# A GELU block with its backward pass: the first block of x loaded plainly and turned by TensorE, u kept out of q's tile, new orders

## The chip, the cores and the metric

The kernel runs on 1 core of one Trainium2 chip. The metric is the device time of one execution in microseconds (us); less is better. The profile is of one further execution on the same chip.

## What is computed

With x and grad_out of 2048 x 448, w1 of 448 x 1792 and w2 of 1792 x 448, all bf16, the reference computes

```python
def _fwd_reference(x, w1, b1, w2, b2):
    h = jnp.einsum("bsd,df->bsf", x, w1) + b1
    h = _gelu(h)
    return jnp.einsum("bsf,fd->bsd", h, w2) + b2
...
    _out, _vjp = jax.vjp(_f, x, w1, b1, w2, b2)
    _grads = _vjp(grad_out)
```

where `_gelu` is the tanh approximation. There are six outputs: out, and the gradients of x, w1, b1, w2 and b2.

## The kernel before

The 2048 rows of x are cut into 4 blocks of 512 and the 1792 hidden columns into 7 pairs of 128-column tiles, so there are 28 pairs p, block by block: pair p belongs to block p // 7. For each pair the kernel does these steps, by the letters of its order lists:

- `u` (TensorE, L315): (x w1) turned, hidden columns on the partitions, 512 rows of x along the free axis, into two PSUM banks. Since 448 = 3.5 x 128, a pair runs as half-array products: `u`p.1 is 6 matmuls of 64 rows, `u`p.2 is 8, and two of them run side by side (L248). For pair 0 the block is halved instead, into `h0.0` and `h1.0`, 8 matmuls of 256 columns each (L278).
- `c` (L399): the two banks plus b1 go to SBUF, tile A on ACT and B on DVE.
- `g`, `s`, `t` on ACT (the GELU, a square, a tanh: L420, L425, L450) and `e r y z m n` on DVE (L430 to L460) make the GELU and its derivative; each works on 1024 elements per partition.
- `q` (L332): (grad_out w2^T) turned, like `u`, from gT and w2T, always into banks 6 and 7, which are one tile, `qb`.
- `G` (L465, DVE): the derivative times q, which frees `qb` for the next pair.
- `o` and `x` (L338): out and the gradient of x, one block at a time, 2 halves x 14 hidden tiles, in banks 0 to 3; `p` is such a unit of 4 matmuls for block 0's out. `vo` and `vx` (L479) evict them into three stages, `S` (L495) stores them.

The hidden activations go to DRAM (`H`, L570), the gradients of the pre-activation are turned on chip by DMA (`T`, L574). After the 28 pairs TensorE runs two long products of 14 x 16 matmuls each, for the gradients of w1 (L704) and w2 (L758).

The order is written out by hand for every engine: PE_ORDER (L91), ACT_ORDER (L112), DVE_ORDER (L119), SP_ORDER (L130), POOL_ORDER (L138). A planner (L18) only adds the waits; nothing is reordered. U_BANK (L137) gives the banks of `u`: pair 1 banks 0 and 1, pair 3 banks 6 and 7 (in `qb`), all others 4 and 5. `h1.0` also lies in 6 and 7 (L321).

The head runs so. SP issues X0.0 and X0.1, two DMA loads that turn x's first block on the way (L510, L537), and then the plain loads of w1 (`L`, and `R` for its last 64 rows: L545, L550) and w2 (`K`, L558), and further turned loads: `Y` of grad_out, `J` of w2, `X` of x, `I` of w1. Eight DMA semaphores go round, so a load waits for the landing of the one eight places before it. ACT issues L0, R0, b1 and b2 and loads its table. TensorE runs 9 idle matmuls (`W9`, L365), spreads b2 over the partitions (`B`, L589), runs one more idle matmul, then h0.0. DVE turns b1 (L606), copies b2 (L634) and one edge column (`Dx0`, L530).

Of the kernel before, what the change touches and what calls it, by code (L numbers as in the profile page):

```python
# [88 lines left out]


PE_ORDER = """  # L91
W9 B W1 h0.0 h1.0 u1.1 u2.1 u1.2 u2.2 u3.1 p0.0 p0.1 u3.2 u4.1 p0.2 p0.3 u4.2 p1.0 p1.1 p1.2 p1.3 p2.0 u5.1 p2.1 p2.2
u5.2 p2.3 p3.0 p3.1 p3.2 u6.1 p3.3 u6.2 q0.1 p4.0 p4.1 q0.2 p4.2 u7.1 p4.3 p5.0 u7.2 p5.1 p5.2 p5.3 u8.1 p6.0 p6.1
u8.2 q1.1 p6.2 p6.3 q1.2 u9.1 o1.1.0.4.1 u9.2 o1.0.0.4.1 q2.1 u10.1 q2.2 u10.2 o1.0.0.4.2 q3.1 u11.1 q3.2 u11.2
o1.1.0.4.2 o1.0.4.8.1 o1.1.4.8.1 u12.1 o1.0.4.8.2 u12.2 q4.1 o1.1.4.8.2 q4.2 u13.1 o1.0.8.11.1 u13.2 q5.1 o1.1.8.11.1
q5.2 o1.0.8.11.2 o1.1.8.11.2 o1.0.11.14.1 o1.1.11.14.1 q6.1 o1.0.11.14.2 q6.2 o1.1.11.14.2 x0.0.0.4.1 u14.1 x0.0.0.4.2
u14.2 x0.1.0.4.1 q7.1 u15.1 q7.2 u15.2 x0.1.0.4.2 x0.0.4.8.1 q8.1 u16.1 q8.2 u16.2 x0.1.4.8.1 x0.0.4.8.2 q9.1 u17.1
q9.2 u17.2 x0.1.4.8.2 x0.0.8.11.1 x0.1.8.11.1 x0.0.8.11.2 u18.1 x0.1.8.11.2 u18.2 q10.1 x0.0.11.14.1 q10.2 u19.1
x0.1.11.14.1 u19.2 q11.1 x0.0.11.14.2 q11.2 u20.1 x0.1.11.14.2 u20.2 q12.1 o2.0.0.4.1 q12.2 o2.1.0.4.1 o2.0.0.4.2
o2.1.0.4.2 o2.0.4.8.1 q13.1 o2.1.4.8.1 q13.2 o2.0.4.8.2 o2.1.4.8.2 o2.0.8.11.1 o2.1.8.11.1 q14.1 o2.0.8.11.2 q14.2  # L100
u21.1 o2.1.8.11.2 u21.2 q15.1 o2.0.11.14.1 q15.2 u22.1 o2.1.11.14.1 u22.2 q16.1 o2.0.11.14.2 u23.1 q16.2 u23.2
o2.1.11.14.2 x1.0.0.4.1 u24.1 x1.0.0.4.2 u24.2 x1.1.0.4.1 q17.1 x1.1.0.4.2 q17.2 x1.0.4.8.1 x1.1.4.8.1 x1.0.4.8.2
q18.1 x1.1.4.8.2 q18.2 x1.0.8.11.1 x1.1.8.11.1 x1.0.8.11.2 q19.1 x1.1.8.11.2 q19.2 x1.0.11.14.1 x1.1.11.14.1
x1.0.11.14.2 u25.1 x1.1.11.14.2 u25.2 q20.1 o3.0.0.4.1 q20.2 o3.1.0.4.1 u26.1 o3.0.0.4.2 u26.2 q21.1 o3.1.0.4.2 q21.2
o3.0.4.8.1 u27.1 o3.1.4.8.1 u27.2 q22.1 o3.0.4.8.2 q22.2 o3.1.4.8.2 o3.0.8.11.1 o3.1.8.11.1 q23.1 o3.0.8.11.2 q23.2
o3.1.8.11.2 o3.0.11.14.1 o3.1.11.14.1 o3.0.11.14.2 q24.1 o3.1.11.14.2 q24.2 x2.0.0.4.1 x2.1.0.4.1 x2.0.0.4.2 q25.1
x2.1.0.4.2 q25.2 x2.0.4.8.1 x2.1.4.8.1 x2.0.4.8.2 x2.1.4.8.2 x2.0.8.11.1 x2.1.8.11.1 x2.0.8.11.2 q26.1 x2.1.8.11.2
q26.2 x2.0.11.14.1 x2.1.11.14.1 x2.0.11.14.2 q27.1 x2.1.11.14.2 q27.2 x3.0.0.4.1 x3.1.0.4.1 x3.0.0.4.2 x3.1.0.4.2
x3.0.4.8.1 x3.1.4.8.1 x3.0.4.8.2 x3.1.4.8.2 x3.0.8.11.1 x3.1.8.11.1 x3.0.8.11.2 x3.1.8.11.2 x3.0.11.14.1 x3.1.11.14.1
x3.0.11.14.2 x3.1.11.14.2  # L110
"""
ACT_ORDER = """  # L112
L0 R0 b1 b2 table c0A0 c0A1 s0 g0 c1A t0 s1 g1 s2 c3A g2 c4A t1 g3 s3 c5A t2 g4 s4 s5 c6A g5 g6 c7A t3 g7 s6 c8A g8
c9A g9 t4 c10A g10 s7 t5 c11A g11 s8 c12A t6 g12 s9 c13A g13 t7 t8 c14A g14 s10 t9 c15A g15 s11 t10 c16A g16 s12 t11
c17A g17 s13 s14 c18A t12 g18 c19A g19 t13 vx0.0 vx0.1 vx0.2 c20A vx0.3 g20 s15 t14 s16 t15 s17 s18 t16 c21A g21 t17
c22A g22 s19 t18 c23A g23 s20 t19 s21 t20 s22 c24A t21 g24 vx1.0 vx1.1 vx1.2 vx1.3 s23 c25A t22 g25 s24 c26A t23 g26
s25 s26 c27A t24 g27 s27 t25 t26 t27 vx2.0 vx2.1 vx2.2 vx2.3 vx3.0 vx3.1 vx3.2 vx3.3
"""
DVE_ORDER = """  # L119
b1T b2c Dx0 c0B0 c0B1 e0 r0 y0 c1B c2A c2B z0 e1 c3B m0 r1 y1 c4B z1 e2 n0 m1 r2 y2 z2 c5B n1 m2 Dg0 n2 c6B G0 e3 r3  # L120
y3 c7B z3 m3 n3 c8B vo0.2 vo0.3 vo0.0 vo0.1 G1 e4 c9B r4 y4 z4 G2 c10B m4 e5 n4 r5 y5 z5 c11B m5 G3 n5 e6 r6 y6 c12B
z6 m6 G4 n6 e7 c13B r7 y7 z7 G5 e8 m7 r8 y8 vo1.0 vo1.1 z8 vo1.2 m8 vo1.3 G6 c14B e9 n7 r9 y9 z9 G7 c15B m9 e10 n8 r10
y10 z10 G8 c16B m10 e11 n9 r11 y11 z11 c17B m11 G9 n10 e12 n11 r12 c18B y12 z12 G10 m12 e13 c19B r13 y13 z13 G11 m13
c20B e14 n12 r14 y14 z14 G12 m14 e15 n13 r15 y15 z15 n14 G13 m15 e16 n15 r16 y16 z16 G14 m16 e17 c21B r17 y17 z17 G15
m17 c22B e18 n16 r18 y18 vo2.0 vo2.1 c23B vo2.2 vo2.3 z18 G16 m18 e19 n17 r19 y19 z19 G17 m19 e20 n18 r20 y20 z20 G18
m20 e21 n19 r21 y21 z21 c24B G19 m21 e22 n20 r22 y22 z22 c25B G20 m22 e23 n21 r23 y23 z23 c26B n22 m23 G21 n23 e24 r24
y24 z24 c27B G22 m24 e25 n24 r25 y25 z25 G23 m25 vo3.0 vo3.1 vo3.2 vo3.3 G24 e26 e27 r26 r27 y26 y27 z26 z27 m26 m27
n25 n26 G25 n27 G26 G27
"""
# [33 lines left out]
def make_plan(tc, ctx, x, w1, b1, w2, b2, grad_out, out_0, out_1, out_2, out_3, out_4, out_5):  # L163
# [420 lines left out]
    for t in PE_ORDER.split():  # L584
        k, a = t[0], t[1:]
        if k == "W":
            wake(int(a))
        elif k == "B":
            pe("b2u", lambda: nc.tensor.matmul(bk_(3)[:, 0:D], lhsT=one[0:1, 0:P], rhs=stage[NST - 1][0:1, 0, :], start=True, stop=True,  # L589
                                               skip_group_check=True), ["b2r"], [bank(("b2u",), 3)], ("s448", 1), (None, 0))  # L590
# [11 lines left out]
    pl.op("POOL", "b1z", lambda: nc.gpsimd.memset(b1n[:], 0.0), [], ["b1z"], ("tiny", 1))
# [199 lines left out]
```

## Time and profile before

| what | value |
|---|---|
| median of 3 runs | 271.16 us (270.48 to 271.91) |
| the profiled execution | 271.01 us |
| its span, from the first to the last instruction | 269.2 us |
| TensorE (PE) busy | 262.0 us, 97% of the span |
| VectorE (DVE) busy | 202.6 us, 75% |
| ScalarE (ACT) busy | 121.3 us, 45% |
| GpSimd (POOL) busy | 15.2 us, 6% |
| moved by DMA | 46.09 MB, mean 171 GB/s |

A line such as L241 is a line of the kernel. PEld is the weight load that runs beside the matmuls. In the lines of groups stand the busy time, the mean of one instruction in ns, then the idle time of the engine just before them and what ended it. The chain of waits is followed back from the last instruction, so it shows at each moment what the end was waiting for.

### The profile page before, as it was taken

What the parts mean: (1) busy time and instruction counts of PE and PEld (TensorE: products, weight loads), DVE (VectorE), ACT (ScalarE), POOL (GpSimd) and SP (SyncE); (2) the same over time, 40 slices, a digit from 0 to 9 for tenths busy, and PEclk for the clock granted to TensorE, in tenths of its full rate; (3) what the DMA queues carried; (4) which work ended last, traced back from release to release, by engine and by line L of the source; (5) the groups of instructions that cost most, each with busy time, mean ns of one, the idle gap of its engine ahead of it and who ended that gap; (6) DMA issues with size and microseconds to landing.
All of it is one profiled execution on the core that took longest, in us unless ns stands there. A gap on an engine that the chain in (4) does not pass through costs nothing.

```text
span 269.2 us, 5316 instructions
## 1 busy us (share of the span) xinstructions
PE 262.0 (97%) x2157; PEld 161.5 (60%) x2157; DVE 202.6 (75%) x286; ACT 121.3 (45%) x153; POOL 15.2 (6%) x9
## 2 busy tenths in 40 slices
...
GB/s 149 281 264 198 192 153 139 230 276 240 233 205 207 171 204 46 121 156 154 56 209 61 255 260 41 215 206 104 162 150 230 186 178 196 190 173 181 68 71 34
DMA packets 121403, 46.09 MB, mean 171 GB/s; under 512 B 98879, under 2 KB 121249, under 8 KB 121378
## 3 DMA queue, kind: packets, MB, share of 16 engines
...
q10 hardware_dynamic: 510, 0.33, 0.4%
...
## 4 chain that ended last, share of the span: by engine, by line
PE 91%; DVE 3%; ACT 2%; DMA 1%; ACTq 1%; issue 0%
PE bank L241 42%; PE qb L241 16%; PE bank L758 12%; PE bank L704 11%; PE qb L704 4%; PE qb L758 4%; DMA st<-in_b_dram 1%; ACT TR L427 1%; DVE gh_nat L411 1%; PE bank L285 1%; DVE TR L442 1%; ACTq L505 1%; PE qb L285 1%; DVE TR L457 0%; DVE TR L447 0%; DVE TR L437 0%
## 5 line engine op out<-in xcount | busy, mean ns | idle before, releaser
L241 PEld LDWEIGHTS <-HG 64*128 64x128 bf16 x896 | 62.1, 94 | 26.9 <-POOLq L236 0.8
L241 PE MATMUL qb<-gT,w2Tf 64*128 64x512 bf16 x392 | 53.7, 376 | 0.0
L241 PE MATMUL bank<-w_sb,HG 64*128 64x448 bf16 x448 | 51.6, 349 | 0.1
L241 PE MATMUL bank<-xT,w1f 64*128 64x512 bf16 x364 | 49.1, 376 | 1.6 <-DVE gh_nat L411 1.6
L241 PE MATMUL bank<-w1T_sb,HG 64*128 64x448 bf16 x448 | 48.2, 349 | 0.0
L467 DVE SCALAR_TENSOR_TENSOR HG<-TR,qb 128x1024 bf16<-128x1024 bf16 x28 | 34.1, 1218 | 7.0 <-PE qb L241 6.8
L241 PEld LDWEIGHTS <-w2Tf 64*128 64x128 bf16 x392 | 27.0, 94 | 13.4
L758 PEld LDWEIGHTS <-HG 128*128 128x128 bf16 x240 | 23.4, 98 | 19.2
L241 PEld LDWEIGHTS <-w1f 64*128 64x128 bf16 x378 | 24.2, 94 | 16.9 <-issue 2.5
L704 PEld LDWEIGHTS <-gh_nat 128*128 128x128 bf16 x224 | 21.8, 98 | 20.6 <-issue 0.4
L452 ACT ACTIVATE TR<-TR 128x1024 bf16<-128x1024 bf16 x28 | 29.3, 1048 | 10.0 <-DVE TR L442 10.0
L758 PE MATMUL bank<-w2Tf,HG 128*128 128x448 bf16 (+1 forms) x176 | 32.3, 344 | 0.0
L704 PE MATMUL bank<-w1f,gh_nat 128*128 128x448 bf16 x160 | 30.8, 353 | 0.0
L727 DVE TENSOR_TENSOR w1T_sb<-w1T_sb,gh_nat 128x1792 f32<-128x1792 f32 x14 | 28.4, 2026 | 0.5
L733 POOL PARTITION_ALL_REDUCE w1T_sb<-w1T_sb x1 | 10.6, 10649 | 206.2 <-DVE w1T_sb L731 206.2
L764 DVE CAST w_sb<-bank 128x448 bf16<-128x448 f32 x5 | 3.1, 625 | 24.8 <-PE bank L758 24.8
L427 ACT ACTIVATE TR<-gh_nat 128x1024 bf16<-128x1024 bf16 x15 | 15.8, 1055 | 10.8 <-DVE TR L462 10.6
L457 DVE TENSOR_SCALAR TR<-TR 128x2048 bf16<-128x2048 bf16 x28 | 19.2, 688 | 0.5 <-ACT TR L452 0.5
L462 DVE TENSOR_TENSOR TR<-TR 128x1024 bf16<-128x1024 bf16 x28 | 19.2, 687 | 0.1
L447 DVE TENSOR_TENSOR TR<-TR,HG 128x1024 bf16<-128x1024 bf16 x28 | 19.1, 685 | 0.0
L427 ACT ACTIVATE TR<-ub 128x1024 bf16<-128x1024 bf16 x13 | 13.7, 1055 | 10.5 <-DVE TR L462 9.9
L742 DVE TENSOR_TENSOR ub<-ub,w2Tf 128x448 f32<-128x448 f32 x14 | 16.4, 1172 | 0.5
...
## 6 DMA issues: line engine op xcount, KB each, us to landing
...
```

Source lines behind the costliest of these rows:

```text
L241: m = nc.tensor.matmul(bk_(b)[:, 0:n], lhsT=l, rhs=r, start=st, stop=sp, skip_group_check=True)
L427: pl.op("ACT", f"s{p}", lambda: nc.scalar.activation(out=TR[p % NTR][:, 1], in_=ubuf(p), func=ACT.Square, scale=sc), [("ub", p)], [v], ("a ...
L447: pl.op("DVE", f"R{p}", lambda: nc.vector.tensor_tensor(out=t[:, 1], in0=t[:, 1], in1=hblk(p), op=ALU.mult), [("r", p), ("h", p)], [val((" ...
L452: pl.op("ACT", f"t{p}", lambda: nc.scalar.activation(out=t[:, 0], in_=t[:, 0], func=ACT.Tanh), [("y", p)], [val(("t", p), ("TR0", p % NTR) ...
L457: pl.op("DVE", f"m{p}", lambda: nc.vector.tensor_scalar(out=t[:], in0=t[:], scalar1=1.0, scalar2=None, op0=ALU.subtract), [("t", p), ("r2" ...
L462: pl.op("DVE", f"n{p}", lambda: nc.vector.tensor_tensor(out=t[:, 0], in0=t[:, 0], in1=t[:, 1], op=ALU.mult), [("m0", p), ("m1", p)], [val( ...
L467: pl.op("DVE", f"G{p}", lambda: nc.vector.scalar_tensor_tensor(out=ghblk(p), in0=t[:, 0], scalar=2.0, in1=qb[:, :, :], op0=ALU.subtract, o ...
L704: nc.tensor.matmul(bk_(bk)[:, 0:D], lhsT=gh_nat[:, st // 4, ft, st % 4, :], rhs=x_nat[:, st, :], start=(st == 0), stop=(st == NS - 1))
L727: nc.vector.tensor_tensor(out=hs3, in0=a, in1=gh_nat[:, st // 4, :, st % 4, :], op=ALU.add)
L733: pl.op("POOL", "gb1", lambda: nc.gpsimd.partition_all_reduce(gb1_w, hsum, channels=P, reduce_op=bass_isa.ReduceOp.add), ["hsc"], ["gb1"], ...
L742: nc.vector.tensor_tensor(out=gsum, in0=gsum, in1=g_nat[:, st, :], op=ALU.add)
L758: nc.tensor.matmul(bk_(bk)[:, 0:d1 - d0], lhsT=h_nat[ft][:, st, :], rhs=g_nat[:, st, d0:d1], start=(st == 0), stop=(st == NS - 1))
```

## The change

x's first block is no longer loaded by turned loads. SP issues three plain loads of its rows (one tile of 128 rows, one, and two) into the third TR buffer, which is free so early; POOL writes column minus row as int32 into a stage, DVE makes an identity of it; TensorE turns each 128 x 128 piece by a product with the identity, 16 matmuls, into banks 0 to 3; DVE copies the first and the third bank into xT, ACT the second and the fourth. R0 moves from ACT to SP. The idle matmuls become 6, ahead of the turns; `B` moves behind h1.0, to bank 6.

No `u` lies in `qb` any more: h1.0 goes to banks 2 and 3, pair 2 to banks 2 and 3, pair 3 to 4 and 5.

All orders are new. From pair 4 on both evictions `c` are ACT's (24 move from DVE). The gradient of x of block 0 runs before the out of block 1, and so on in turn; q0 comes behind u5 instead of u6; the units of `o` and `x` take 5, 5 and 4 hidden tiles instead of 4, 4, 3 and 3. In SP's order `K3` moves behind `Y0` and `J0`, and `I0` and `I1` come before `Y1`.

```diff
 PE_ORDER = """
-W9 B W1 h0.0 h1.0 u1.1 u2.1 u1.2 u2.2 u3.1 p0.0 p0.1 u3.2 u4.1 p0.2 p0.3 u4.2 p1.0 p1.1 p1.2 p1.3 p2.0 u5.1 p2.1 p2.2
-u5.2 p2.3 p3.0 p3.1 p3.2 u6.1 p3.3 u6.2 q0.1 p4.0 p4.1 q0.2 p4.2 u7.1 p4.3 p5.0 u7.2 p5.1 p5.2 p5.3 u8.1 p6.0 p6.1
...
+W6 X0 X1 X2 X3 h0.0 h1.0 B u1.1 u2.1 u1.2 u3.1 u2.2 u3.2 p0.0 p0.1 u4.1 p0.2 p0.3 u4.2 p1.0 p1.1 p1.2 p1.3 u5.1 p2.0
+p2.1 u5.2 q0.1 p2.2 p2.3 q0.2 u6.1 p3.0 p3.1 u6.2 q1.1 p3.2 p3.3 q1.2 p4.0 p4.1 p4.2 p4.3 u7.1 p5.0 p5.1 u7.2 p5.2
+q2.1 p5.3 p6.0 q2.2 u8.1 p6.1 p6.2 u8.2 q3.1 p6.3 x0.1.0.5.1 u9.1 q3.2 u9.2 x0.0.0.5.1 x0.1.0.5.2 q4.1 u10.1 q4.2
+u10.2 x0.0.0.5.2 q5.1 x0.0.5.10.1 u11.1 q5.2 u11.2 x0.1.5.10.1 q6.1 u12.1 q6.2 u12.2 x0.0.5.10.2 x0.1.5.10.2 u13.1
+q7.1 u13.2 q7.2 x0.0.10.14.1 x0.1.10.14.1 x0.0.10.14.2 u14.1 q8.1 u14.2 q8.2 x0.1.10.14.2 o1.0.0.5.1 u15.1 q9.1 u15.2
+q9.2 o1.1.0.5.1 u16.1 q10.1 u16.2 q10.2 o1.0.0.5.2 u17.1 o1.1.0.5.2 u17.2 o1.0.5.10.1 o1.1.5.10.1 q11.1 u18.1 q11.2
...
 ACT_ORDER = """
-L0 R0 b1 b2 table c0A0 c0A1 s0 g0 c1A t0 s1 g1 s2 c3A g2 c4A t1 g3 s3 c5A t2 g4 s4 s5 c6A g5 g6 c7A t3 g7 s6 c8A g8
...
+L0 b1 b2 table X1 X3 c0A0 c0A1 s0 g0 c1B s1 c2A c3A s2 g1 g2 c4A c4B g3 g4 t0 c5A c5B t1 s3 g5 t2 s4 c6A c6B t3 g6 s5
+c7A s6 c7B t4 g7 c8A c8B g8 s7 t5 c9A c9B g9 s8 t6 c10A c10B g10 s9 t7 c11A c11B g11 s10 t8 c12A c12B g12 s11 t9 c13A
...
 DVE_ORDER = """
-b1T b2c Dx0 c0B0 c0B1 e0 r0 y0 c1B c2A c2B z0 e1 c3B m0 r1 y1 c4B z1 e2 n0 m1 r2 y2 z2 c5B n1 m2 Dg0 n2 c6B G0 e3 r3
...
+ident X0 X2 Dx0 b1T c0B0 c0B1 b2c e0 r0 c1A z0 y0 c2B c3B e1 r1 y1 e2 z1 r2 y2 z2 Dg0 m0 n0 G0 m1 e3 n1 r3 y3 m2 z3 G1 n2
...
 SP_ORDER = """
-X0.0 X0.1 L1 R2 L2 K1 K0 R1 R3 L3 K2 K3 Y0 J0 X1 J2 J1 Y1 J3 I1 I0 Ex Eg So0.1 So0.0 X2 H0 H1 H2 H3 H4 H5 H6 H7 H8 T0
...
+xr01 xr12 xr24 R0 L1 R2 L2 K1 R1 K0 R3 L3 K2 Y0 J0 K3 J1 X1 J2 I0 J3 I1 Y1 Ex Eg So0.1 X2 So0.0 H0 H1 H2 H3 H4 H5 H6
...
-U_BANK = {1: 0, 3: 6}
+U_BANK = {1: 0, 2: 2}
...
-            bk, hs, c, tag = ((4, 5), (6, 7))[hf], (hf,), (256 * hf, 256 * hf + 256), f"h{hf}"
+            bk, hs, c, tag = ((4, 5), (2, 3))[hf], (hf,), (256 * hf, 256 * hf + 256), f"h{hf}"
...
+    x_rows = TR[NTR - 1][:, :, :, :].rearrange("p a h s -> p (a h) s")
+    ident = stage[0][:, 0, 0:P]
+    diff = stage[1][:, 0, 0:2 * P].bitcast(mybir.dt.int32)
+
+    def LXN(t0, t1, eng="SP"):
+
+        src = bass.AP(tensor=x2.tensor, offset=x2.offset + t0 * P * D, ap=[[D, P], [P * D, t1 - t0], [1, 4 * P]])
+        dma(eng, f"xrows{t0}", x_rows[:, t0:t1, :], src, [], [("xrows", t // 2) for t in range(t0, t1)], (t1 - t0) * 131072)
+
+    def identity():
+        nc.vector.tensor_scalar(out=ident, in0=diff, scalar1=0.0, scalar2=None, op0=ALU.is_equal)
+
+    def XT(t):
+
+        def fn():
+            for k in range(4):
+                nc.tensor.matmul(bk_(t)[:, k * P:(k + 1) * P], lhsT=x_rows[:, t, k * P:(k + 1) * P], rhs=ident,
+                                 start=True, stop=True, skip_group_check=True)
+        pe(f"xt{t}", fn, [("xrows", t // 2), "ident"], [bank(("xt", t), t)], ("s128", 4), (None, 0))
+
+    def XC(t, eng):
+        out = xT[0][:, :, EDGE + t * P:EDGE + (t + 1) * P]
+        src = bk_(t)[:, :].rearrange("p (k s) -> p k s", k=4)
+        fn = (lambda: nc.scalar.copy(out=out, in_=src)) if eng == "ACT" else (lambda: nc.vector.tensor_copy(out=out, in_=src))
+        pl.op(eng, f"xc{t}", fn, [("xt", t)], [val(("xT", 0, t // 2), ("xT", 0, t // 2))], ("copy", 512))
...
+    pl.op("POOL", "diff", lambda: nc.gpsimd.iota(diff, pattern=[[1, P]], base=0, channel_multiplier=-1), [], ["diff"], ("tiny", 1))
```

In the instruction order that comes of it, one ISA instruction stands on POOL directly ahead of the iota (the old order has one such instruction ahead of the first of its two partition reduces, L733); the two small loads of w2's last rows follow the iota on POOL.

More of the change, by code (lines that the diff above doesn't have):

```diff
@@ L91 @@
 PE_ORDER = """
-W9 B W1 h0.0 h1.0 u1.1 u2.1 u1.2 u2.2 u3.1 p0.0 p0.1 u3.2 u4.1 p0.2 p0.3 u4.2 p1.0 p1.1 p1.2 p1.3 p2.0 u5.1 p2.1 p2.2
-u5.2 p2.3 p3.0 p3.1 p3.2 u6.1 p3.3 u6.2 q0.1 p4.0 p4.1 q0.2 p4.2 u7.1 p4.3 p5.0 u7.2 p5.1 p5.2 p5.3 u8.1 p6.0 p6.1
-u8.2 q1.1 p6.2 p6.3 q1.2 u9.1 o1.1.0.4.1 u9.2 o1.0.0.4.1 q2.1 u10.1 q2.2 u10.2 o1.0.0.4.2 q3.1 u11.1 q3.2 u11.2
-o1.1.0.4.2 o1.0.4.8.1 o1.1.4.8.1 u12.1 o1.0.4.8.2 u12.2 q4.1 o1.1.4.8.2 q4.2 u13.1 o1.0.8.11.1 u13.2 q5.1 o1.1.8.11.1
-q5.2 o1.0.8.11.2 o1.1.8.11.2 o1.0.11.14.1 o1.1.11.14.1 q6.1 o1.0.11.14.2 q6.2 o1.1.11.14.2 x0.0.0.4.1 u14.1 x0.0.0.4.2
@@ L97 @@
[L97 to L110, printed above, removed]
+W6 X0 X1 X2 X3 h0.0 h1.0 B u1.1 u2.1 u1.2 u3.1 u2.2 u3.2 p0.0 p0.1 u4.1 p0.2 p0.3 u4.2 p1.0 p1.1 p1.2 p1.3 u5.1 p2.0
+p2.1 u5.2 q0.1 p2.2 p2.3 q0.2 u6.1 p3.0 p3.1 u6.2 q1.1 p3.2 p3.3 q1.2 p4.0 p4.1 p4.2 p4.3 u7.1 p5.0 p5.1 u7.2 p5.2
@@ new lines @@
+q2.1 p5.3 p6.0 q2.2 u8.1 p6.1 p6.2 u8.2 q3.1 p6.3 x0.1.0.5.1 u9.1 q3.2 u9.2 x0.0.0.5.1 x0.1.0.5.2 q4.1 u10.1 q4.2
+u10.2 x0.0.0.5.2 q5.1 x0.0.5.10.1 u11.1 q5.2 u11.2 x0.1.5.10.1 q6.1 u12.1 q6.2 u12.2 x0.0.5.10.2 x0.1.5.10.2 u13.1
+q7.1 u13.2 q7.2 x0.0.10.14.1 x0.1.10.14.1 x0.0.10.14.2 u14.1 q8.1 u14.2 q8.2 x0.1.10.14.2 o1.0.0.5.1 u15.1 q9.1 u15.2
+q9.2 o1.1.0.5.1 u16.1 q10.1 u16.2 q10.2 o1.0.0.5.2 u17.1 o1.1.0.5.2 u17.2 o1.0.5.10.1 o1.1.5.10.1 q11.1 u18.1 q11.2
+u18.2 o1.0.5.10.2 o1.1.5.10.2 o1.0.10.14.1 u19.1 o1.1.10.14.1 u19.2 q12.1 o1.0.10.14.2 q12.2 u20.1 o1.1.10.14.2 u20.2
@@ new lines @@
+q13.1 x1.0.0.5.1 q13.2 x1.1.0.5.1 x1.0.0.5.2 x1.1.0.5.2 q14.1 x1.0.5.10.1 q14.2 x1.1.5.10.1 x1.0.5.10.2 x1.1.5.10.2
+u21.1 q15.1 u21.2 q15.2 x1.0.10.14.1 u22.1 x1.1.10.14.1 u22.2 q16.1 x1.0.10.14.2 q16.2 u23.1 x1.1.10.14.2 u23.2
+o2.0.0.5.1 q17.1 u24.1 q17.2 u24.2 o2.1.0.5.1 o2.0.0.5.2 o2.1.0.5.2 o2.0.5.10.1 o2.1.5.10.1 q18.1 o2.0.5.10.2 q18.2
+o2.1.5.10.2 o2.0.10.14.1 q19.1 o2.1.10.14.1 q19.2 o2.0.10.14.2 u25.1 o2.1.10.14.2 u25.2 q20.1 x2.0.0.5.1 q20.2
+x2.1.0.5.1 x2.0.0.5.2 x2.1.0.5.2 u26.1 q21.1 u26.2 q21.2 x2.0.5.10.1 u27.1 x2.1.5.10.1 u27.2 q22.1 x2.0.5.10.2 q22.2
@@ L111 @@
+x2.1.5.10.2 x2.0.10.14.1 x2.1.10.14.1 q23.1 x2.0.10.14.2 q23.2 x2.1.10.14.2 o3.0.0.5.1 q24.1 o3.1.0.5.1 q24.2
+o3.0.0.5.2 o3.1.0.5.2 q25.1 o3.0.5.10.1 q25.2 o3.1.5.10.1 o3.0.5.10.2 o3.1.5.10.2 q26.1 o3.0.10.14.1 q26.2
+o3.1.10.14.1 o3.0.10.14.2 o3.1.10.14.2 q27.1 x3.0.0.5.1 q27.2 x3.1.0.5.1 x3.0.0.5.2 x3.1.0.5.2 x3.0.5.10.1 x3.1.5.10.1
+x3.0.5.10.2 x3.1.5.10.2 x3.0.10.14.1 x3.1.10.14.1 x3.0.10.14.2 x3.1.10.14.2
 """
 ACT_ORDER = """
-L0 R0 b1 b2 table c0A0 c0A1 s0 g0 c1A t0 s1 g1 s2 c3A g2 c4A t1 g3 s3 c5A t2 g4 s4 s5 c6A g5 g6 c7A t3 g7 s6 c8A g8
@@ L114 @@
[L114 to L117, printed above, removed]
+L0 b1 b2 table X1 X3 c0A0 c0A1 s0 g0 c1B s1 c2A c3A s2 g1 g2 c4A c4B g3 g4 t0 c5A c5B t1 s3 g5 t2 s4 c6A c6B t3 g6 s5
@@ new lines @@
+c7A s6 c7B t4 g7 c8A c8B g8 s7 t5 c9A c9B g9 s8 t6 c10A c10B g10 s9 t7 c11A c11B g11 s10 t8 c12A c12B g12 s11 t9 c13A
+c13B g13 vx0.0 s12 vx0.1 t10 c14A c14B vx0.2 vx0.3 g14 s13 c15A c15B t11 g15 c16A c16B t12 s14 g16 s15 c17A c17B t13
+g17 s16 c18A c18B g18 t14 c19A c19B s17 g19 c20A c20B g20 t15 s18 t16 s19 t17 c21A c21B s20 g21 c22A c22B t18 vx1.0
+vx1.1 g22 vx1.2 c23A c23B s21 vx1.3 g23 t19 t20 s22 s23 c24A c24B t21 g24 s24 c25A c25B t22 g25 c26A c26B s25 g26 t23
+t24 c27A c27B s26 s27 g27 t25 vx2.0 vx2.1 vx2.2 vx2.3 t26 t27 vx3.0 vx3.1 vx3.2 vx3.3
@@ L118 @@
 """
 DVE_ORDER = """
-b1T b2c Dx0 c0B0 c0B1 e0 r0 y0 c1B c2A c2B z0 e1 c3B m0 r1 y1 c4B z1 e2 n0 m1 r2 y2 z2 c5B n1 m2 Dg0 n2 c6B G0 e3 r3
[L121 to L128, printed above, removed]
+ident X0 X2 Dx0 b1T c0B0 c0B1 b2c e0 r0 c1A z0 y0 c2B c3B e1 r1 y1 e2 z1 r2 y2 z2 Dg0 m0 n0 G0 m1 e3 n1 r3 y3 m2 z3 G1 n2
@@ new lines @@
+m3 e4 n3 r4 y4 z4 G2 m4 vo0.2 vo0.3 e5 n4 r5 vo0.0 z5 vo0.1 y5 G3 m5 e6 n5 r6 y6 z6 G4 m6 e7 n6 r7 y7 z7 G5 m7 e8 n7
+r8 y8 z8 G6 m8 e9 n8 r9 y9 z9 m9 G7 n9 e10 r10 y10 z10 m10 G8 n10 e11 r11 y11 z11 G9 e12 m11 r12 y12 z12 n11 G10 m12
+e13 n12 r13 y13 z13 m13 n13 G11 e14 r14 y14 z14 m14 n14 vo1.0 vo1.1 G12 vo1.2 vo1.3 e15 r15 y15 z15 G13 m15 e16 n15
+r16 y16 z16 m16 G14 n16 e17 r17 y17 z17 m17 n17 G15 e18 r18 y18 z18 G16 m18 e19 n18 r19 y19 z19 G17 e20 m19 r20 y20
+z20 n19 m20 n20 G18 e21 r21 y21 z21 G19 vo2.0 m21 vo2.1 vo2.2 vo2.3 e22 n21 r22 y22 z22 G20 e23 r23 m22 z23 y23 n22
@@ L129 @@
+G21 e24 r24 y24 z24 m23 n23 m24 n24 G22 e25 r25 y25 z25 m25 G23 n25 e26 r26 y26 z26 G24 m26 e27 n26 r27 y27 z27 G25
+m27 n27 G26 vo3.0 vo3.1 vo3.2 vo3.3 G27
 """
 SP_ORDER = """
-X0.0 X0.1 L1 R2 L2 K1 K0 R1 R3 L3 K2 K3 Y0 J0 X1 J2 J1 Y1 J3 I1 I0 Ex Eg So0.1 So0.0 X2 H0 H1 H2 H3 H4 H5 H6 H7 H8 T0
-T1 H9 T2 H10 T3 H11 T4 H12 T5 H13 So1.0 So1.1 T6 H14 T7 H15 T8 Y2 H16 X3 T9 H17 T10 H18 Sx0.0 H19 T11 Sx0.1 H20 T12
-T13 T14 H21 T15 So2.0 H22 Y3 So2.1 H23 T16 T17 T18 T19 Sx1.0 Sx1.1 H24 T20 H25 Nx T21 H26 T22 H27 T23 So3.0 So3.1 T24
```

27 lines of the change are left out of this document (21 added, 6 removed).

## The prediction

> **What bounds the kernel now.** I read the chain of work that ended last first, because a sum of busy time does not say where time can still be won. These are its pieces where the head of the kernel gives way to the rest, and its end.
>
> ```profile
> 7.49 1.82 PE bank L285 x8
> 9.30 1.40 PE qb L285 x7
> ...
> 16.50 0.95 ACT HG L422
> 17.45 0.95 ACT TR L427
> 18.39 0.58 ACT gh_nat L409
> ...
> 26.30 0.04 issue
> 26.34 2.07 PE bank L241 x18
> 28.41 0.65 PE qb L241 x6
> 29.05 0.76 PE bank L241 x8
> 29.81 0.86 PE qb L241 x8
> ...
> 170.58 10.59 PE bank L241 x112
> ...
> 264.53 1.55 PE bank L758 x16
> 266.08 0.02 issue
> ```
>
> The columns are start, length, piece. From 26.34 to 266.08 every piece is TensorE: it waits for nothing in those 239.7 us. Before that the chain runs through ACT and DVE. So a gain can only come from the first 26 us or from less matmul work. The pieces also price the work: a `u` or `q` of one pair is 0.65 (6 matmuls) plus 0.86 (8), 1.51 us; 8 matmuls of an `o` or `x` unit are 0.76, so a `p` of 4 is 0.38.
>
> How much idle does the head hold? From the end of the second half of pair 0 (h1.0, 9.30 + 1.40 = 10.70) to u6.1 (26.34) lie 15.64 us. The order puts u1 to u5 (5 x 1.51 = 7.55) and 15 `p` (15 x 0.378 = 5.67) there: 13.2 us. So TensorE idles 2.4 us after h1.0, and h1.0 itself ends late. That is all that the new order can win.
>
> The timeline shows why pair 0 is late:
>
> ```profile
> 0.73 2.70 SPq L517 DMA_TRANSPOSE xT<-in_x_dram  x2
> 0.73 0.20 POOL L602 MEMSET b1n<- 32x128 bf16 x1 [0.29 <-POOLq L786]
> ...
> 0.77 4.00 PE L368 MATMUL bank<-const-bfloat16-1.0 128*128 128x512 bf16 x9 [0.77 <-PEq L786]
> ...
> 3.47 1.83 SPq L505 DMA_DIRECT2D w1f<-in_w_dram  x3
> ...
> 6.42 0.53 PE L589 MATMUL bank<-st,const-bfloat16-1.0 1*128 1x448 bf16 x1 [1.65 <-DMA st<-in_b_dram]
> ...
> 7.28 2.03 PE L285 MATMUL bank<-xT,w1f 128*128 128x256 bf16 x8
> ...
> 9.34 0.48 DVE L411 TENSOR_SCALAR ub<-bank,b1T 128x256 bf16<-128x256 f32 x1 [1.45 <-PE bank L285]
> ```
>
> SyncE needs 2.70 us merely to issue the two turned loads, against 0.61 for a plain one (1.83 / 3). TensorE stands behind the `b2` row until 6.42 and starts pair 0 at 7.28. The loads of the head land so (size, then us from issue to landing):
>
> ```profile
> w1f<-in_w_dram ACTq DMA_DIRECT2D x1, 192.0 KB, 2.7
> ...
> w1f<-in_w_dram SPq DMA_DIRECT2D x1, 128.0 KB, 5.3
> xT<-in_x_dram SPq DMA_TRANSPOSE x2, 5.0
> ```
>
> The profiled execution took 271.01 us for a span of 269.2 (1.8 lie around it) and is 0.15 under the median of 271.16. Sums are made against 271.0, and 0.15 is added at the end.
>
> **The change, part by part.** *The rows of x.* Three plain loads from 0.73 on, 0.61 apart: issued at 0.7, 1.3 and 2.0. Plain loads took 2.7 to 5.3; I take 2.7 for the first two, which meet an almost idle DMA, and 3.4 for the third, twice as large: 3.4, 4.0, 5.4. R0 (from ACT) and L1 go behind them on SP, issued at 2.6 and 3.2, earlier than L1 in the old order (3.47), so no weight is late.
>
> *The identity.* It adds a wait at the front of two engines. POOL writes an iota behind the memset that ends at 0.93; DVE compares it with 0, behind which stand its copies X0 and X2, the edge, `b1T` and c0B0; TensorE's X0 waits for DVE, with the whole of TensorE behind it. No row shows an iota. In the changed instruction order an ISA instruction stands ahead of it, of the kind that stands ahead of the first partition reduce and nowhere else in the old one. So the nearest rows are POOL's:
>
> ```profile
> 208.85 10.65 POOL L733 PARTITION_ALL_REDUCE w1T_sb<-w1T_sb  x1 [206.20 <-DVE w1T_sb L731]
> 226.26 2.88 POOL L744 PARTITION_ALL_REDUCE ub<-ub  x1 [6.76 <-DVE ub L742]
> ```
>
> The lower end is the memset's 0.20. The upper end is the first reduce, 10.65, the only operation in its place; it is 7.77 above the second, which has a quarter of the columns and no such instruction ahead (if time went with columns alone, four times 2.88 would explain all of it). I take 6.0 for the iota with what stands ahead of it, a little above the middle of 0.20 and 10.65, because the row nearest to it in kind is the longer one. The identity is then there at 0.9 + 6.0 + 0.2 (the compare, half the columns of the 0.48 in the timeline) = 7.1, while the rows lie ready.
>
> The Trainium skill, GPSIMD Engine Reference, section 2.1, states that the first call of a freshly loaded GpSimd kernel pays some 6 us (5.95 measured) without a visible instruction; no row of before separates it. By that figure alone the identity comes at 7.1 and the sum below is the same.
>
> *The 16 turns.* Prices:
>
> ```profile
> L285 PEld LDWEIGHTS <-w1f 128*128 128x128 bf16 x12 | 1.6, 142 | 1.2 <-issue 0.7
> ...
> L409 ACT ACTIVATE gh_nat<-bank,b1T 128x512 bf16<-128x512 f32 x14 | 9.5, 678 | 5.0 <-PE bank L241 4.8
> ...
> L411 DVE TENSOR_SCALAR gh_nat<-bank,b1T 128x512 bf16<-128x512 f32 x14 | 10.5, 748 | 0.7 <-PE bank L241 0.5
> ...
> L427 ACT ACTIVATE TR<-gh_nat 128x1024 bf16<-128x1024 bf16 x15 | 15.8, 1055 | 10.8 <-DVE TR L462 10.6
> ```
>
> h0.0 took 1.82 for 8 matmuls of 256 columns, 0.228 each; a turn has 128 columns and a 0.142 weight load, so 0.114 to 0.228; I take 0.15: 0.6 per block of rows, 2.4 in all. A block is copied out in 0.75 (DVE) or 0.68 (ACT). From 7.1: the turns end at 9.5, h0.0 runs behind them to 11.35, X3 is copied at 9.7 to 10.4 beside it, h1.0 takes 1.4 to 1.82 (1.65) and ends at 13.0. Against 10.70 that is **+2.3**.
>
> The clock belongs here. The wake's 512 columns took 4.00 / 9 = 0.44 each, h0.0 0.228 per 256, a late `u` 0.65 / 3 = 0.216 per two matmuls of 512 columns, side by side on half the rows each: half pace until about 10 us, though this row shows a granted clock of 1.00 (the column behind POOL):
>
> ```profile
> 0.00:7.28 7.28, 4.86 (x12) 1.43 (x12) 1.00 (x5) 1.49 (x2) 1.73 (x7) 1.00 0.76 142
> ```
>
> The new wake of 6 ends near 3.4 and, with the identity at 7.1, 3.7 us of silence follow. The Trainium skill, TensorE: Matmul & The Clock Gate, Part 1, gives full pace after some 3.4 us of sustained activity and half pace again after an idle window; the trace agrees for the start (nine wakes, a gap, half pace). By it h1.0 runs at half pace too, 0.2 above my sum.
>
> *The order behind h1.0.* Up to u9.1 TensorE now has u1 to u8 (12.1), 28 `p` (10.6), q0 to q2 and q3.1 (5.2) and one x unit of 10 matmuls (0.95): 28.8 us. From c4 on both evictions of a pair are ACT's. ACT must do by then, from c0A1 (0.48) on, 20 activations of 1024 (each 0.95 in the chain's spacing to 1.05 alone) and 13 evictions (0.58 to 0.68): 27.0 to 30.3 us. DVE loses 24 evictions of 0.75. So ACT takes the place of DVE and lies within 2 us of TensorE. Idle of TensorE there: at least some 0.5, at most 2.0; I take 1.2 where before has 2.4: **-1.2**. The clean bounds are 0.4 and 1.9 won.
>
> *At nothing.* The units of 5, 5 and 4 instead of 4, 4, 3 and 3: 112 matmuls take 10.59, 0.189 per pair, so the borders cost nothing that could be saved. No `u` in the tile of q: q0.1 ran at 28.41, long after the old u3 was evicted. Less DVE work behind 26 us: TensorE waited for none of it. The iota's successors on POOL, the `w2` ends, are needed by a turned load at 33 us, cover of 20 us.
>
> Sum: 271.0 + 2.3 - 1.2 = 272.1, with 0.15 272.3.
>
> **The rivals.** *The identity is in time: the change does what it says.* For it: a memset on POOL takes 0.20, the first reduce may be all columns. Against it: the instruction ahead of the iota. The turns then follow the loads: X0 at 3.5, X1 at 4.1, X2 and X3 from 5.4 to 6.7, X3 copied by 7.4, X1 by 5.5; h0.0 5.5 to 7.3, h1.0 to 9.0, 1.7 before 10.70. 271.0 - 1.7 - 1.2 + 0.15 = **268.3**; with 1.9 won behind h1.0 and a warmer h1.0, 267. It breaks even with before when the identity comes some 2.9 us behind the first rows, at 6.3.
>
> *ACT holds up the evictions (slower).* Each u from u4 on waits for two evictions in a row on one engine, 1.36, in one pair of banks. At u9, u12, u13, u16, u17, u24 and u27 the order leaves TensorE under 2 us between (u12: an x unit 0.95 and q6.1 0.65, 1.60). If ACT stands in an activation of 1.05 when the pair ends, u12 loses 1.05 + 1.36 - 1.60 = 0.8. Seven such are 5.6: 272.3 + 5.6 = **278**, from an early identity 274. Against it: ACT's 4.4 us a pair (3 x 1.05 and 2 x 0.68, less the spacing) against TensorE's 6.0, so it mostly waits at the eviction. It decides from 0.1 us per place on, if the identity is late.
>
> **How the numbers follow.** Late identity 0.53, at 272.3 with 270.5 to 274 (its price from 4.5 to 7.8); in time 0.37, 267 to 269; ACT 0.10. The measurement tells about 0.5%, 1.36 us: faster is below 269.8, slower above 272.5. The late identity is split by that: 0.03 faster, 0.54 same, 0.43 slower; in time is 0.93 faster; ACT is slower. Faster 0.36, same 0.31, slower 0.33. The range that leaves out 0.2 runs from 266.9 to 274.0; the forecast's own is 270.5 to 274.
>
> **What would show it.** The start of the iota and of DVE's compare: 7 for the forecast, under 2 for the first rival. The end of h1.0: 13.0 or 9.0. No TensorE wait longer than 0.3 us between u9.1 and the end; waits for ACT L409 at u12, u13 or u24 would show the second rival. I am wrong if the compare starts between 3 and 6, or if the idle behind h1.0 exceeds 2.4.

## The result, and the profile after

The changed kernel took 273.2 us in the median (13 runs, 272.37 to 275.09), the kernel before 270.87 us on the same chip (13 runs, 269.57 to 271.91). The ratio is 1.0091 with a 95% interval of 1.0069 to 1.0114: slower by 0.9%. The forecast was 272.3 us. Executions that took over 1.5% longer than the fastest of their kernel are left out of the ratios in this document, but not out of its medians.

The profiled execution of after took 273.2 us for a span of 271.4. Its chain of waits (start, length, piece):

```profile
0.72 0.19 POOL b1n L632
...
0.98 8.24 issue
9.22 0.24 POOL st L633
...
9.49 0.24 DVE st L549
...
9.77 1.86 PE bank L555 x16
11.63 3.00 PE bank L282 x16
...
14.73 0.49 DVE ub L411
...
19.11 0.58 ACT ub L409
...
19.74 7.10 PE bank L238 x68
...
268.29 0.02 issue
```

In before the chain of the head ran through the `b2` row and pair 0. Here its longest piece is `issue`: 8.24 us in which POOL waited for nothing that the profile shows, just ahead of the iota. Then follow the compare (L549), the 16 turns (L555) and pair 0 (L282), without a gap. Pair 0 ends at 14.63; in before at 10.70. From 14.63 to the end of TensorE at 268.29 lie 253.7 us; in before, from 10.70 to 266.08, 255.4. So the head lost 3.9 us and the order behind it won 1.7: together a loss of 2.2, which is 273.2 less 271.0.

The timeline of after shows who stood ready meanwhile (the bracket is the engine's idle time before, and what ended it):

```profile
0.73 1.34 SPq L507 DMA_DIRECT2D TR<-in_x_dram  x3
...
0.77 2.72 PE L365 MATMUL bank<-const-bfloat16-1.0 128*128 128x512 bf16 x6 [0.77 <-PEq L823]
...
3.40 0.10 PEld L555 LDWEIGHTS <-TR 128*128 128x128 bf16 x1 [0.82 <-DMA TR<-in_x_dram]
...
9.22 0.23 POOL L633 IOTA st<- 128x128 int32 x1 [8.30 <-issue]
...
9.49 0.23 DVE L549 TENSOR_SCALAR st<-st 128x128 bf16<-128x128 int32 x1 [9.49 <-POOL st L633]
9.77 1.86 PE L555 MATMUL bank<-st,TR 128*128 128x128 bf16 x16 [6.29 <-DVE st L549]
```

The iota itself takes 0.23 us; 8.30 pass before it. The first rows of x are there at 3.40, when TensorE loads them as weights for the first turn. TensorE stands for 6.29 us, from the last idle matmul on. Its waits, first those of before over the first 30 us, then those of after:

```profile
PE bank L589 <- DMA st<-in_b_dram: 1.7, 1, 1.7
PE bank L241 <- DVE gh_nat L411: 1.6, 2, 1.2
```

```profile
PE bank L555 <- DVE st L549: 6.3, 1, 6.3
...
PE bank L238 <- ACT ub L409: 0.2, 1, 0.2
```

The waits for `b2` and for DVE's evictions are gone, and ACT, which now evicts everything from pair 4 on, holds TensorE for 0.2 us in all. One wait of 6.3 has taken their place.

### The profile page after: what moved, and what is told of

The parts are those of the page before. It is cut to its first block, busy times and chain, and to the rows that moved or that the text cites. A ratio compares the mean times of both kernels' runs of the same rounds, so it can differ in the third digit from the quotient of the medians.

```text
span 271.4 us, 5313 instructions
## 1 busy us (share of the span) xinstructions
PE 261.0 (96%) x2169; PEld 190.5 (70%) x2169; DVE 190.0 (70%) x264; ACT 135.5 (50%) x180; POOL 15.4 (6%) x10
## 3 DMA queue, kind: packets, MB, share of 16 engines
HBM read 7.68 MB, written 14.27 MB: 81 GB/s over the span
## 4 chain that ended last, share of the span: by engine, by line
PE 93%; issue 3%; ACT 1%; DVE 1%; POOL 0%; ACTq 0%; DVEq 0%; POOLq 0%
PE bank L238 45%; PE qb L238 16%; PE bank L795 12%; PE bank L741 11%; PE qb L741 4%; PE qb L795 4%; PE bank L282 1%; ACT TR L427 1%; PE bank L555 1%; DVE ub L411 0%; ACT ub L409 0%; DVE TR L432 0%; DVE TR L437 0%; ACT w_sb L800 0%; POOL st L633 0%
## 5 line engine op out<-in xcount | busy, mean ns | idle before, releaser
L238 PEld LDWEIGHTS <-HG 64*128 64x128 bf16 x896 | 74.2, 94 | 14.4 <-POOLq L233 0.7
L238 PE MATMUL qb<-gT,w2Tf 64*128 64x512 bf16 x392 | 57.9, 376 | 0.0
L238 PE MATMUL bank<-xT,w1f 64*128 64x512 bf16 x378 | 54.0, 376 | 0.0
L238 PE MATMUL bank<-w_sb,HG 64*128 64x448 bf16 x448 | 52.3, 349 | 0.2 <-ACT ub L409 0.2
L238 PE MATMUL bank<-w1T_sb,HG 64*128 64x448 bf16 x448 | 49.7, 349 | 0.0
L238 PEld LDWEIGHTS <-w2Tf 64*128 64x128 bf16 x392 | 35.7, 94 | 5.9
L238 PEld LDWEIGHTS <-w1f 64*128 64x128 bf16 x378 | 32.8, 94 | 6.9 <-DMA w_sb<-in_w_dram 0.2
L409 ACT ACTIVATE gh_nat<-bank,b1T 128x512 bf16<-128x512 f32 x29 | 18.3, 677 | 4.2 <-PE bank L238 4.2
L409 ACT ACTIVATE ub<-bank,b1T 128x512 bf16<-128x512 f32 (+1 forms) x24 | 14.9, 666 | 9.2 <-DVE TR L442 4.1
```

Source lines behind the costliest of these rows:

```text
L238: m = nc.tensor.matmul(bk_(b)[:, 0:n], lhsT=l, rhs=r, start=st, stop=sp, skip_group_check=True)
L409: fn = lambda: nc.scalar.activation(out=out, in_=src, func=ACT.Identity, bias=bias)
```

## The experiments

Ratios are to the kernel before on the same chip (medians 270.6 to 270.9 us), with 95% intervals. Of the order lists the edits show only the first words of a line.

**The identity without the iota.** DVE makes it: a ramp by doubling, four 32 x 32 transposes, four compares. POOL has no iota.

```diff
-        nc.vector.tensor_scalar(out=ident, in0=diff, scalar1=0.0, scalar2=None, op0=ALU.is_equal)
+        nc.vector.memset(ident, 0.0)
+        nc.vector.memset(ramp[:, 0:1], 0.0)
+        for n in (1, 2, 4, 8, 16):
+            nc.vector.tensor_scalar(out=ramp[:, n:2 * n], in0=ramp[:, 0:n], scalar1=float(n), scalar2=None, op0=ALU.add)
+        for a in range(4):
+            q = slice(32 * a, 32 * a + 32)
+            nc.vector.transpose(out=rampT[q, :], in_=ramp[0:32, :])
+        for a in range(4):
+            q = slice(32 * a, 32 * a + 32)
+            nc.vector.tensor_tensor(out=ident[q, q], in0=ramp[q, :], in1=rampT[q, :], op=ALU.is_equal)
...
-    pl.op("POOL", "diff", lambda: nc.gpsimd.iota(diff, pattern=[[1, P]], base=0, channel_multiplier=-1), [], ["diff"], ("tiny", 1))
```

> The changed kernel with one difference: the identity is made on VectorE (a ramp by doubling, 32x32 turns, compares), and no iota is on GpSimd. Theory (the wait for the iota, some 8.2 us in which GpSimd runs nothing, is the whole loss): the compare ends before 3.5, the turns follow the rows, the end of h1.0 comes near 9.0 instead of 14.6, and as nothing behind it changes the time falls by 5 to 6 us to 267.2 to 268.2, 1.0% to 1.4% under the kernel before. Rival (the turns on TensorE and the new orders themselves cost the time): no less than 271.

Measured: 268.5 us, ratio 0.9921 (0.9891 to 0.9952). The timeline of this kernel, TensorE:

```profile
3.72 1.19 PE L564 MATMUL bank<-st,TR 128*128 128x128 bf16 x8 [0.24 <-DVE st L558]
5.06 1.03 PE L564 MATMUL bank<-st,TR 128*128 128x128 bf16 x8 [0.15 <-DMA TR<-in_x_dram]
5.89 3.84 PE L282 MATMUL bank<-xT,w1f 128*128 128x256 bf16 x16
```

The turns start at 3.72 instead of 9.77, and nobody waits for long. So the late identity is the whole loss and more: without it the rest of the change wins 0.8%. Pair 0 runs at 0.24 a matmul (3.84 for 16), where other heads below need 0.14 (2.22 for 16); I call the two half and full pace. So it ends at 9.7 and not at 9.0, and the time falls by 4.7, less than expected.

**An iota that nobody reads, in before.**

```diff
+    diff = stage[1][:, 0, 0:2 * P].bitcast(mybir.dt.int32)
+    pl.op("POOL", "diff", lambda: nc.gpsimd.iota(diff, pattern=[[1, P]], base=0, channel_multiplier=-1), [], ["diff"], ("tiny", 1))
```

> The kernel before with one difference: the same iota on GpSimd behind the b1 memset, which nothing reads. Theory (the price is GpSimd's own, paid at the instruction ahead of the iota): the iota starts near 9.2 here too, the two loads of w2's last rows slip behind it and are still in time for 33 us, and the time stays that of before within 0.5%. Rival (the iota was late because something else in the changed head held GpSimd): the iota starts before 2.

Measured: 270.75 us, ratio 0.9988 (0.9959 to 1.0016). POOL's timeline:

```profile
8.50 0.23 POOL L605 IOTA st<- 128x128 int32 x1 [7.59 <-issue]
```

The gap belongs to POOL, not to the changed head, and costs nothing where nobody waits for it. TensorE in the same execution, which took 268.98:

```profile
6.56 1.14 PE L285 MATMUL bank<-xT,w1f 128*128 128x256 bf16 x8
7.63 1.04 PE L285 MATMUL qb<-xT,w1f 128*128 128x256 bf16 x7
```

Here pair 0, in the orders of before, runs at full pace; in the profiled execution of before (271.01) it ran at half. The ten runs of this kernel lie in two groups, three at 268.65 to 268.98 and seven at 270.45 to 271.03. So executions of one order can lie some 2 us apart. Between these two profiles it is the head: pair 0 starts 0.7 earlier and, at full pace, ends 1.9 earlier (8.8 against 10.7). That the pace makes the two groups is not shown, but differences of 1 us between medians below can hold some of it.

**What the gap is.** The first of two kernels leaves both partition reduces out; the gradients of b1 and b2 then hold one partition's own sums.

```diff
-    pl.op("POOL", "gb1", lambda: nc.gpsimd.partition_all_reduce(gb1_w, hsum, channels=P, reduce_op=bass_isa.ReduceOp.add),
+    pl.op("DVE", "gb1", lambda: nc.vector.tensor_copy(out=gb1_w, in_=hsum),
...
-    after(pl.op("POOL", "gb2", lambda: nc.gpsimd.partition_all_reduce(gb2_w, gsum, channels=P, reduce_op=bass_isa.ReduceOp.add),
+    after(pl.op("DVE", "gb2", lambda: nc.vector.tensor_copy(out=gb2_w, in_=gsum),
```

> After, with the two partition reduces left out: the gradients of b1 and b2 then hold one partition's own sums, copied by DVE. The ISA instruction ahead of the iota stays, and nothing else runs on POOL but a memset, the iota and DMA issues. Theory A: the 8.3 us ahead of the iota are a fetch that is needed because the reduces displaced the iota's code in the execution before. Then the iota starts before 2 us, h1.0 ends near 9.5 and the time is about 268.5. Theory B: the gap is paid in every execution, whatever ran before. Then the iota starts at 8 to 9.5 us again and the time stays at 272.5 to 273.5.

Measured: 268.77 us (3 runs), ratio 0.9912 (0.9881 to 0.9944). POOL and TensorE in its timeline:

```profile
0.98 0.23 POOL L633 IOTA st<- 128x128 int32 x1
...
3.30 0.63 PE L555 MATMUL bank<-st,TR 128*128 128x128 bf16 x4
...
6.65 2.22 PE L282 MATMUL bank<-xT,w1f 128*128 128x256 bf16 x16
```

The same ISA instruction stands ahead of the iota, yet the gap is gone: the iota starts at 0.98, and pair 0 ends at 8.9. It seems that what stands 200 us later in the program decides what the head pays. The second kernel keeps the reduces and puts a small iota behind them:

```diff
+    pl.op("POOL", "lib", lambda: nc.gpsimd.iota(b1n[:, :].bitcast(mybir.dt.int32), pattern=[[1, P // 2]], base=0, channel_multiplier=-1),
+          ["gb2"], ["lib"], ("tiny", 1))
```

> After, whole, with one more small iota on POOL behind the second partition reduce, whose values nobody reads; in the instruction order it has an ISA instruction of its own ahead. Theory: the 8.3 us ahead of the head's iota are the fetch of its code, which the reduces at the end of the execution before have displaced; with an iota as the last one, the code is in place when the next execution begins. Then the head's iota starts before 2 us, a gap of some 8 us appears ahead of the one at the end (where 30 us of TensorE's work hide it), h1.0 ends near 9 and the time is 268.2 to 269.5. Rival: nothing stays from one execution to the next, and the gap was absent without the reduces for another reason. Then the head's iota starts at 8.5 to 9.5 and the time is 272.5 to 273.5.

Its POOL timeline:

```profile
1.22 0.23 POOL L633 IOTA st<- 128x128 int32 x1 [0.29 <-issue]
...
208.81 10.62 POOL L770 PARTITION_ALL_REDUCE w1T_sb<-w1T_sb  x1 [206.06 <-DVE w1T_sb L768]
226.19 2.88 POOL L781 PARTITION_ALL_REDUCE ub<-ub  x1 [6.75 <-ACT w_sb L802]
236.75 0.18 POOL L783 IOTA b1n<- 32x64 int32 x1 [7.68 <-DMA out_dram<-gT]
```

The head's iota starts at 1.22, and 7.68 us of idle stand ahead of the one at the end, beside TensorE's last products (the row names a DMA as what ended them; the length is that of the gap in the head). So the gap comes where an iota follows a reduce, and it makes no difference whether the execution ends between them. That it is a fetch of the iota's code, which the reduce has displaced, is the reading that fits; no row shows the fetch itself.

The times of this kernel do not agree among themselves. Six of 12 lie at 268.06 to 269.78, six at 271.77 to 273.03, four of them in the range of after; the ratio 0.9947 (0.9908 to 0.9986) holds one of the upper six. An execution that follows a run of the kernel before, whose last POOL work is a reduce, would find the iota's code displaced; that this makes the upper group is argued, not shown, since no profile of one was taken. Against it: none of the three runs of the kernel without reduces lies there, and one of six of the kernel without any iota does (272.56), so such times have another cause too. The profiled execution (269.78; its pair 0 ends at 8.0) lost something else besides: the windows by stage give its granted clock (after "PE busy") as 0.72 between 10 and 16 us, and 1.00 in the kernel without reduces. The first row is of the kernel with the second iota:

```profile
10.00:16.00 6.00, 5.54 (x36) 0.72 1.14 283
```

```profile
10.00:16.00 6.00, 5.41 (x50) 1.00 1.15 281
```

That is 36 matmuls against 50 in the same 6 us. It also waits 1.4 us for the lower rows of w1, where the other waits 0.5.

**The pace behind a late identity.** After with 20 idle matmuls instead of 6.

```diff
-W6 X0 X1 X2 X3 h0.0 h1.0 B
+W20 X0 X1 X2 X3 h0.0 h1.0 B
```

> After with 20 idle matmuls instead of 6, so that TensorE is busy from 0.8 to between 7 and 9.7 us while it waits for the identity. If half of the loss is the pace of the late turns and of pair 0 (1.86 for 16 turns and 3.0 for 16 matmuls of pair 0, at full pace about 1.0 and 1.9), this gives back up to 2 us: 271.2. If the wait for the iota is all, and the pace behind it no different, the time stays at 273.2, with h1.0 ending at 14.6.

Measured: 271.81 us, ratio 1.0046 (1.0017 to 1.0075). Its timeline:

```profile
9.04 0.23 POOL L633 IOTA st<- 128x128 int32 x1 [8.12 <-issue]
...
9.58 1.05 PE L555 MATMUL bank<-st,TR 128*128 128x128 bf16 x16 [1.41 <-DMA w1f<-in_w_dram]
10.86 2.22 PE L282 MATMUL bank<-xT,w1f 128*128 128x256 bf16 x16 [0.23 <-ACT xT L562]
```

(The row of the turns names a DMA as what ended the idle time; DVE's compare ended at 9.53, just ahead of them.) The turns fall from 1.86 to 1.05 and pair 0 from 3.00 to 2.22. Of the some 4.4 us that the late identity costs (273.2 against 268.8, medians) some 1.4 are the pace that TensorE lost in the silence; the other 3 are the wait.

**The parts of the change that do win.** Four kernels. First, before with the `b2` product behind pair 0:

```diff
-W9 B W1 h0.0 h1.0 u1.1
+W9 W1 h0.0 h1.0 B u1.1
...
-b1T b2c Dx0 c0B0 c0B1 e0
+b1T Dx0 c0B0 c0B1 b2c e0
```

> Before, with the product that spreads b2 put behind h1.0, and its copy on DVE behind c0B1; nothing else changed. Theory: in before TensorE waited until 6.4 us for the b2 row while the turned rows of x lay ready from 5.7, so h0.0 starts at 6.6 or earlier and the time falls by 0.7 to 1.2 us: 269.4 to 269.9. Rival: before is bound behind h1.0 by DVE and ACT, and what is won in pair 0 is lost there: 270.4 to 270.9.

Measured: 269.48 us, ratio 0.9962 (0.9938 to 0.9986): about 1.0 us won (0.4 to 1.7) by moving one matmul and the copy behind it. TensorE:

```profile
5.71 1.14 PE L285 MATMUL bank<-xT,w1f 128*128 128x256 bf16 x8 [1.02 <-DMA xT<-in_x_dram]
6.78 1.15 PE L285 MATMUL qb<-xT,w1f 128*128 128x256 bf16 x8
```

Pair 0 starts at 5.71 with the turned load; in before at 7.28. This profiled execution took 270.69, over a microsecond more than the median: between 12 and 14 us its granted clock was 0.50. Second, all of after's orders and banks with the turned load and no identity:

```diff
-W6 X0 X1 X2 X3 h0.0 h1.0 B
+W9 h0.0 h1.0 B
...
-ident X0 X2 Dx0 b1T c0B0
+b1T Dx0 c0B0
...
-xr01 xr12 xr24 R0 L1
+X0.0 X0.1 L1
```

(R0 goes back to ACT, and ACT's copies X1 and X3 go.)

> The changed kernel with the head's loads put back: two turned loads of x, no rows, no identity, no turns, R0 on ACT, 9 idle matmuls; all orders and the banks as changed, so the b2 product stands behind h1.0. Theory (the turned load was not what held pair 0 up, the b2 row ahead of it was): h0.0 starts at 5.8 instead of 7.3, h1.0 ends near 9.3, and with the 1.7 us won behind it the time is 267.5 to 268.5, the same as with the identity on VectorE. Rival (the turned load is what holds pair 0): h1.0 ends near 10.7 as before, time 269 to 269.5.

Measured: 268.93 us, ratio 0.9946 (0.9922 to 0.9971). Third, the reverse: before's orders and banks with the plain rows, the identity by DVE, and `b2` behind pair 0.

> The other half: the orders and banks of the kernel before, but the head with the plain loads, the identity made on VectorE, the 16 turns, R0 on SP and the b2 product behind h1.0. Theory (the orders behind h1.0 are worth 1.7 us, the earlier pair 0 another 1.7): time 269.0 to 269.5 against 270.9 before. Rival (the new orders win nothing by themselves, the end of the head follows pair 0): the same time as the changed kernel with the identity on VectorE, 267.5 to 268.

Measured: 269.89 us, ratio 0.9973 (0.9939 to 1.0007). So with the plain head the new orders win about 0.5% by the ratios (0.9973 to 0.9921), 1.4 us, though the two intervals overlap a little; with the turned head (0.9962 to 0.9946) no step is clear. Nor is the plain head clearly ahead of the turned one: 0.9921 against 0.9946 with the new orders, 0.9973 against 0.9962 with the old. Fourth, the second kernel with 12 idle matmuls instead of 9:

> The changed orders with turned loads of x (as in the run before of that name), with 12 idle matmuls instead of 9, so that TensorE has no silence of 0.8 us ahead of h0.0. If the pace of TensorE from 5.5 to 13.5 us is held at half by that silence, full pace comes some us earlier and the time is 267 to 268. If it isn't, the idle matmuls end at 6.1 and push h0.0 back by 0.5: 269 to 269.5.

Measured: 268.67 us, ratio 0.9908 (0.9882 to 0.9934). Its TensorE, and then that of the second kernel:

```profile
5.72 2.22 PE L282 MATMUL bank<-xT,w1f 128*128 128x256 bf16 x16
...
10.87 4.06 PE L238 MATMUL bank<-xT,w1f 64*128 64x512 bf16 x36 [1.69 <-DMA w1f<-in_w_dram]
```

```profile
5.56 3.91 PE L282 MATMUL bank<-xT,w1f 128*128 128x256 bf16 x16 [0.80 <-DMA xT<-in_x_dram]
...
9.88 6.49 PE L238 MATMUL bank<-xT,w1f 64*128 64x512 bf16 x42
```

Pair 0 runs at full pace instead of half; the 1.5 us that this wins stand again as a wait of 1.69 for the lower rows of w1, and the `u` behind it win some 1.6 by their pace. That is the difference between these two executions, 268.71 and 270.26. But the profiled one of the second kernel is among its slower ones: four of its 12 runs lie at 270.10 to 270.26, the median at 268.93. So between the kernels no step is clear (268.93 to 268.67), and that the three more idle matmuls make the pace is not shown. The row with the wait names the next edit, made to the fourth kernel: R2 issued by ACT behind R0.

```diff
-L0 R0 b1 b2 table c0A0
+L0 R0 R2 b1 b2 table c0A0
...
-X0.0 X0.1 L1 R2 L2 K1
+X0.0 X0.1 L1 L2 K1
```

> The changed orders with turned loads of x and 12 idle matmuls, with the load R2 (the lower 64 rows of w1 for the first 1024 columns) issued by ACT behind R0 instead of by SP behind L1. Theory: behind pair 0 TensorE now waits 1.7 us for that load, which lands at 10.9; issued at about 2 us it lands before 8, the wait goes and the time falls from 268.7 to 267.0 to 267.8. Rival: the idle only moves to the first p, which needs the GELU of pair 0 from ACT (whose first work is issued behind this load): 268.4 to 268.9.

Measured: 268.17 us, ratio 0.9902 (0.9871 to 0.9933), the fastest median here and under both kernels, though no clear step from 268.67, and between the two forecasts. The wait fell, but not to nothing:

```profile
10.03 4.06 PE L238 MATMUL bank<-xT,w1f 64*128 64x512 bf16 x36 [0.51 <-DMA w1f<-in_w_dram]
14.28 1.05 PE L238 MATMUL bank<-w_sb,HG 64*128 64x448 bf16 x8 [0.19 <-ACT ub L406]
```

Pair 0 itself now ends 0.5 later (8.5): TensorE waits 0.27 and 0.24 for its halves of xT, presumably since more loads run beside them.

## Why the prediction was right, and where its terms were off

The mechanism forecast, an identity that comes late while the rows lie ready, is what happened, and the experiments show it: with the identity early the same change gives 268.5 and 268.8. The size was short: a loss of 1.1 was forecast, and 2.3 came. Step by step:

- **The identity.** The mis-sized term. The iota with what stands ahead was put at 6.0, the identity at 7.1; the gap and the iota took 8.5 and it came at 9.73, 2.6 later. The price lay over the forecast's own range for it (4.5 to 7.8), under the upper bound 10.65. What bounded it was read wrongly: the first reduce's 10.65 against 2.88 holds no such gap. In after, where the reduce follows an iota, it takes 10.62 too; so its length goes with its columns, four times as many. The 6.0 was a choice between two bounds that had nothing to do with what happened, and that the time still fell into the forecast's range is in part luck: the next two terms came out better. The Trainium skill, GPSIMD Engine Reference, section 2.1, has 5.95 us for the first call of a freshly loaded kernel; here the gap, if it is the same thing, was 8.30, 8.12, 7.59 and 7.68, and at most 0.3 where the last operation before it was an iota. The measurement decides.
- **Turns and pair 0.** 5.9 us from identity to the end of h1.0 were forecast, 4.9 measured (9.77 to 14.63). The 16 turns took 1.86, not 2.4: 0.116 each, at the lower end of the bounds. Pair 0 took 3.00, not 3.5. This won back 1.0, so the head lost 3.9 instead of 2.3.
- **Behind h1.0.** 1.2 was forecast with bounds of 0.4 and 1.9; 1.7 measured. TensorE has one wait of 0.2 left there, and none is listed in all the rest of the execution.
- **The sum.** 271.0 + 3.9 - 1.7 = 273.2. The identity 2.6 later, the turns and pair 0 1.0 shorter and 0.5 more won behind them leave 1.1 over the sum of 272.1; the 0.15 added at the end makes it 0.9 over 272.3.
- **The rival in time**, at 268.3: with the iota's gap gone 268.8, by DVE 268.5. Its price was right to 0.5; pair 0 ended at 8.9 and 9.7, where 9.0 was written.
- **The rival of ACT's evictions** did not occur: 0.2 us of waiting for ACT in all.
- **At nothing.** Right for after, where the wait hid it: "no weight is late" holds since TensorE comes to u1 at 14.8. With an early pair 0 the lower rows of w1, landing at 10 to 11, are the next wait. That the place of `b2` was worth about 1.0 us by itself was not priced at all.
- **The clock.** By the Trainium skill, TensorE: Matmul & The Clock Gate, Part 1, silence costs the full pace; the run with 20 idle matmuls agrees, and prices it at 1.4. The 0.2 that was written is for h1.0 alone: turns and h0.0 stood in the sum at slow prices already. The some 3.4 us of sustained activity that the Trainium skill has there do not cover the run with the identity by DVE, where TensorE was busy from 0.77 with no gap over 0.24 and still ran pair 0, from 5.89 to 9.7, at half pace. They do not cover the head of before either, which the prediction took as agreeing: nine idle matmuls made TensorE busy for 4.00 us, the gap behind them was 1.65, and pair 0 ran at half pace.
